# One list of SBUF places for z, its sums and its split parts, with splits issued five steps ahead, in a fused attention and two-FFN kernel

## The chip, the cores and the metric

The kernel runs on one core of one Trainium2 chip. The metric is device microseconds (us) of one execution. TensorE (PE in the profile; PEld is its weight load) multiplies, VectorE (DVE) and ScalarE (ACT) do the elementwise work, SyncE (SP) issues nearly all DMAs. Every engine runs its own instructions in program order.

## The reference

```
attn: x (8,8,512,64), state (8,8,32,64)
  xread = softmax(x @ state.T / 8) @ state ; sread = softmax(state @ x.T / 8) @ x
  tokens = concat(xread, sread) per batch: 8 x (512 + 32) = 4352 rows of 512
moe:  h = tokens @ w_in (512x2048); y = leaky_relu(h, 0.01) @ w_out (2048x512)
moe2: z = silu(y @ w_gate) * (y @ w_val)   (512x1536 each)
      out = z @ w_out2                     (1536x512), 4352 x 512 float32
```

## The kernel before

**Layer 1** (up to 695 us) does attention and the first FFN for eight blocks of 512 tokens and one tail block of 256 state rows, and leaves y in DRAM. Beside it, `convert` and `finish2` prepare the second FFN's weights: `stage` loads a 512 KB tile of 64-bit words (`ws`), `to_f32` turns it into float32 (`two`), `finish2` forms sums of quadrants and splits each value into a high and a low part (`hl`), which go to `quad_dram`. For w_out2 (key "o") `stage` issues four DMAs, which also reorder the columns in runs of 32.

**Layer 2** handles the blocks in four pairs (i, j). All products are float32 values as high and low parts, three matmuls for a product of two 128-wide pieces (`multiply` or `passes`: low x high, high x low, high x high). A pair's matrix product is done by seven products in place of eight (steps p, s, q, b, r, a, c of sums of quadrants), and each has two stages:

- `quads(f)`, f = 0 to 5 (HF = 6): the gate and value products of the column tiles f and f + 6, from `yc` (the sums of y, split), 13 steps in the order ORDER2; each step is 6 matmuls. `keep` (ACT) copies a bank to a temporary C, `add` (DVE, L801) adds a bank to it, `gate_out` and `val_out` make z. `last_product(f)` is step c of gate and value; its matmuls continue in the bank X of steps p, q, r, so they wait until `add` of step r has read that bank. `z_sum` makes sums of z (u).
- `read_out`: out = z @ w_out2, 42 steps (seven steps times six f), 6 matmuls each. `split_next(n + 2)` issues the split (`split_h` on ACT makes zh, `split_l` on DVE makes zl) of the operand that step n + 2 multiplies; zh and zl have three buffers each. Where a chain ends (f = 5), the two banks are copied to C (p, s, q), or, for b, r, a, added to C (two DVE adds) and turned by two 32x32-block transposes into `ost`, which four DMAs store; for c the banks are turned directly. Step n = 0 is followed by `last_product(5)`.

`y_sums` makes the next pair's `yc`: it loads y (`yr`), and on each call makes one to three casts (ACT), differences and low parts (DVE). In `read_out`, `others(n)` calls it at every second step (the third read-out at most steps before 28, then `tail`). `Places` is a list of SBUF tags: `take` uses the oldest free one, `give` returns it. The weights `wq` are loaded 16 places ahead by SP.

The order of all engines is the order in which this code issues.

Of the kernel before, what the change touches and what calls it, by code (L numbers as in the profile page):

```python
# [25 lines left out]
def kernel(  # L26
# [612 lines left out]
    def y_sums(pair, take, give):  # L639
# [32 lines left out]
        for k in range(2):  # L672
            b = raw_b[k]
            high(0, k, b["B0"])
            t4 = sub(b["B3"], b["B0"])
            yield
            high(1, k, b["B1"])
            low(0, k, b["B0"])
            yield
            high(2, k, b["B2"])  # L680
            t6 = sub(b["B2"], b["B3"], b["B3"])
            yield
            high(4, k, t4)
            low(2, k, b["B2"], False)
            yield
            t5 = sub(b["B2"], t4, b["B2"])
            high(6, k, t6)
            if k == 0:
                raw_b.append({"B0": load(i, 1), "B3": load(j, 1)})
            yield  # L690
            high(5, k, t5)
            low(4, k, t4)
            yield
            low(1, k, b["B1"], False)
            t7 = sub(b["B1"], t5, b["B1"])
            if k == 0:
                raw_b[1] |= {"B1": load(i, 3), "B2": load(j, 3)}
            yield
            high(7, k, t7)
            low(5, k, t5)  # L700
            yield
            low(6, k, t6)
            low(7, k, t7)
            yield
# [3 lines left out]
    ORDER3 = "psqbrac"  # L708

    def order_of_products():  # L710
        for p in pairs:
# [10 lines left out]
            for step in ORDER3:  # L722
                for f in range(HF):
                    yield "o", f, step
                    if (step, f) == (ORDER3[0], 0):
                        yield from (("gate", HF - 1, "c"), ("val", HF - 1, "c"))
# [19 lines left out]
    def layer2(p2, ps2):  # L746
# [30 lines left out]
        Zt, Zu = {}, {}  # L777

        def z_sum(n, f):

            if n == 0:
                Zu[f] = p2.tile([P, 2, S], F32, tag=f"u{f}", name="u", bufs=1)
            t1, t2 = Zu[f][:, 0], Zu[f][:, 1]
            i, j = Zt[f][:, 0], Zt[f][:, 1]
            i2, j2 = (Zt[f + HF][:, 0], Zt[f + HF][:, 1]) if n else (None, None)
            out, a, b = [(t1, j, i), (t2, j2, t1), (j, j2, j), (t2, i2, t2)][n]
            nc.vector.tensor_tensor(out=out, in0=a, in1=b, op=ALU.subtract)

        def z_operand(step, f):
            return {  # L790
                "p": Zt[f][:, 0], "s": Zu[f][:, 0], "q": Zu[f][:, 1], "b": Zt[f + HF][:, 1],
                "r": Zt[f][:, 1], "a": Zt[f + HF][:, 0], "c": Zu[f][:, 1],
            }[step]
# [15 lines left out]
        def val_out(sg, c, f, half):  # L809
            if f not in Zt:  # L810
                Zt[f] = p2.tile([P, 2, S], F32, tag=f"z{f}", name="z", bufs=1)
            nc.vector.tensor_tensor(out=Zt[f][:, half, :], in0=c, in1=sg[0], op=ALU.mult)
# [66 lines left out]
        def split_z(key, src):  # L879
            z = zs[key] = tuple(p2.tile([P, S], F32R, tag=t, name=t, bufs=3) for t in ("zh", "zl"))  # L880
            split_h(z[0], src)
            split_l(z[1], src, z[0])
# [3 lines left out]
        def split_next(n):  # L886
            if n < len(order_o):
                step, f = order_o[n]
                split_z((step, f), z_operand(step, f))
                if step == "q":  # L890
                    z_sum(3, f)
# [3 lines left out]
        def quadrant_out(block, half, parts, tags, store):  # L895

            o = wres.tile([P, S // 32, 2, 32], F32, tag=f"wr{14 + stored[0] % 2}", name="ost", bufs=1)
            stored[0] += 1
            for d, src in enumerate(parts):
                nc.vector.transpose(out=o[:, :, d, :], in_=src)  # L900
            for q in range(4):
                c = half * 256 + 64 * q
                store[q % len(store)].dma_start(
                    out=out[block * SB:block * SB + S, c:c + 64].rearrange("(g t) c -> t g c", t=32),
                    in_=o[32 * q:32 * (q + 1)].rearrange("t g d c -> t g (d c)"),
                )
# [16 lines left out]
        def read_out(p, others):  # L923

            i, j = pairs[p]
            B_, K = {}, {}
            for n, (step, f) in enumerate(order_o):
                split_next(n + 2)
                w, tag = weights_of("o", f, step)
                zh, zl = zs.pop((step, f))  # L930
                chain_of = {"q": "p", "r": "p", "c": "p", "b": "s"}.get(step, step)
                if chain_of not in B_:
                    B_[chain_of] = [banks.take("ps_o") for _ in range(2)]
                for d in range(2):

                    wh, wl = w[:, 0, d * P:(d + 1) * P], w[:, 1, d * P:(d + 1) * P]
                    todo = [(wl, zh), (wh, zl), (wh, zh)]
                    for m, (a, v) in enumerate(todo):
                        nc.tensor.matmul(  # L939
                            B_[chain_of][d][0], lhsT=a, rhs=v, start=chain_of == step and f == 0 and m == 0,  # L940
                            stop=step in "abc" and f == HF - 1 and m == 2, skip_group_check=True,
                        )
                used(tag)
                if n == 0:
                    last_product(HF - 1)
                    z_sum(1, HF - 1)
                    z_sum(2, HF - 1)
                if f == HF - 1:
# [3 lines left out]
                    elif step == "c":  # L952
                        last = p + 1 == len(pairs)
                        quadrant_out(i, 1, bank, (), (nc.sync, nc.scalar) if last else (nc.sync,))
                    else:
                        kept = K.pop({"a": "p", "b": "q", "r": "s"}[step])
                        for c, t in zip(kept, bank):
                            add(c, t)
                        block, half = {"a": (i, 0), "b": (j, 0), "r": (j, 1)}[step]
                        quadrant_out(block, half, [c for c, _ in kept], (), (nc.sync,))  # L960
                        temps.give(*(t for _, t in kept))
                    if step in "abc":
                        banks.give(*(t for _, t in B_.pop(chain_of)))
                if n:
                    others(n)

        def tail():
# [35 lines left out]
            y = []  # L1003
            for k in range(2):
                t, tag = yr[k]
                parts = p2.tile([P, 2, 2 * n], F32R, tag=f"z{k}", name="yt", bufs=1)
                split_h(parts[:, 0, :], t)
                split_l(parts[:, 1, :], t, parts[:, 0, :])
                temps.give(tag)
                y += [(parts[:, 0, d * n:(d + 1) * n], parts[:, 1, d * n:(d + 1) * n]) for d in range(2)]  # L1010
# [13 lines left out]
            def hidden(f):  # L1024
# [14 lines left out]
                z = zs[f, 2] = tuple(p2.tile([P, S], F32R, tag=t, name=t, bufs=3) for t in ("zh", "zl"))  # L1039
                split_h(z[0][:, :n], sg[:, :n])  # L1040
                split_l(z[1][:, :n], sg[:, :n], z[0][:, :n])
# [10 lines left out]
            for f in range(NF2):  # L1052
# [7 lines left out]
                zh, zl = zs.pop((f, 2))  # L1060
# [6 lines left out]
                wtiles[0].give(*tags)  # L1067
                load2("o", f + 2)
                if f + 2 >= NF2:
                    held[0] = False  # L1070
# [6 lines left out]

        def first_z():
            for n in range(2):
                yield  # L1080
                split_next(n)

        for p in range(len(pairs)):
# [3 lines left out]
            for f in range(HF):  # L1087
# [3 lines left out]
                quads(f, first_z() if f == HF - 1 else iter(()))  # L1091
            tail_steps = tail() if p + 2 == len(pairs) else iter(())

            def others(n):
                if p + 2 == len(pairs):
                    if n < 28:
                        for _ in range(1 if n % 8 else 0):
                            next(sums_y, None)
                    elif n < 39:
                        next(tail_steps)  # L1100
                elif n % 2:
                    next(sums_y, None)

            read_out(p, others)
            for kept in (Zt, Zu):
                kept.clear()
# [3 lines left out]
    with tc.manual_schedule():  # L1110
# [64 lines left out]
        def finish2():  # L1175
# [4 lines left out]
            for m in range(len(keys2) // 2):  # L1180
# [5 lines left out]
                if kind == "o":  # L1186
                    a = [t[:, 0, 0:256], t[:, 1, 0:256], t[:, 0, 256:512], t[:, 1, 256:512]]
                    raws = [t[:, :, 0:256], t[:, :, 256:512]]
# [5 lines left out]

                def sums(out, x, y, op=ALU.subtract):
                    nc.vector.tensor_tensor(out=out, in0=x, in1=y, op=op)
# [17 lines left out]
                for n, two_raw in zip((0, 2), raws):  # L1214
                    hl = halves()
                    split_h(hl[:, :, 0].bitcast(F32R), two_raw)
                    yield 0.05
                    split_l(hl[:, :, 1].bitcast(F32R), two_raw, hl[:, :, 0])
# [350 lines left out]
```

## Time and profile before

| | |
|---|---|
| median of three executions | 1462.88 us (1462.82 to 1463.76) |
| profiled execution | 1462.61 us, of which 1460.8 us span |
| granted TensorE clock, mean | 0.999 of full speed (2.4 GHz) |
| layer 1, to the first product of layer 2 | 0 to 695.8 us |
| layer 2: stages of one pair, quads / read-out | 111.5 us / 66.4 us |
| the second FFN on the tail block | 1229.5 to 1281 us |

A row of a group tells count (x), busy time and mean; a row of the timeline tells start, length, engine, line, operation, what it writes and reads, and in brackets how long the engine sat idle before it and which instruction ended that wait. Lines are those of the kernel before.

### The profile page before, as it was taken

What the parts mean: (1) busy time and instruction counts of PE and PEld (TensorE: products, weight loads), DVE (VectorE), ACT (ScalarE), POOL (GpSimd) and SP (SyncE); (2) the same over time, 40 slices, a digit from 0 to 9 for tenths busy, and PEclk for the clock granted to TensorE, in tenths of its full rate; (3) what the DMA queues carried; (4) which work ended last, traced back from release to release, by engine and by line L of the source; (5) the groups of instructions that cost most, each with busy time, mean ns of one, the idle gap of its engine ahead of it and who ended that gap; (6) DMA issues with size and microseconds to landing.
All of it is one profiled execution on the core that took longest, in us unless ns stands there. A gap on an engine that the chain in (4) does not pass through costs nothing.

```text
span 1460.8 us, 21155 instructions
## 1 busy us (share of the span) xinstructions
PE 1417.8 (97%) x7386; PEld 1123.2 (77%) x7386; DVE 971.0 (66%) x1721; ACT 742.0 (51%) x1335; POOL 3.0 (0%) x8
## 2 busy tenths in 40 slices
PE   5999999999999999999999999999999999999998
PEld 1445777777777777888888778887788878988876
DVE  6877678676777685543555875558665697545575
ACT  6877656666656565644433543336433364333353
POOL 0000000000000000000000000000000000000000
PEclk9999999999999999999999999999999999999999
DMA  8895656667666765551667676676866767876664
GB/s 288 296 317 194 216 203 243 208 223 237 224 219 225 197 188 187 202 181 37 213 193 222 208 218 206 194 224 206 222 203 194 222 198 217 253 262 194 193 187 112
DMA packets 213593, 307.59 MB, mean 211 GB/s; under 512 B 73840, under 2 KB 100464, under 8 KB 212464
## 3 DMA queue, kind: packets, MB, share of 16 engines
q1 hardware_dynamic: 211280, 297.60, 64.9%
q10 hardware_dynamic: 2208, 8.65, 1.5%
q8 instruction: 59, 0.97, 0.3%
q14 instruction: 46, 0.38, 0.1%
HBM read 225.44 MB, written 80.74 MB: 210 GB/s over the span
## 4 chain that ended last, share of the span: by engine, by line
PE 82%; DVE 10%; ACT 3%; DMA 3%; issue 1%; SPq 1%; DVEq 0%; ACTq 0%
PE ps_y L451 22%; PE ps_x L770 16%; PE ps_h L451 13%; PE ps_s L770 9%; PE ps_o L939 9%; PE ps_a L770 4%; DVE zl L167 3%; PE ps_t L451 2%; PE ps_sw L475 2%; DVE C L801 2%; PE ps_yt L451 2%; ACT zh L164 1%; PE ps_s L326 1%; PE ps_o L451 1%; DVE ost L900 1%
## 5 line engine op out<-in xcount | busy, mean ns | idle before, releaser
L451 PE MATMUL ps_y<-gh,w_parts 128*128 128x512 f32 x1024 | 339.7, 392 | 0.0
L770 PE MATMUL ps_x<-yc,wq 128*128 128x512 f32 x1152 | 279.2, 390 | 3.2 <-DVE C L801 3.2
L770 PEld LDWEIGHTS ps_x<-yc,wq 128*128 128x128 f32 x1152 | 215.9, 188 | 49.4 <-DVE C L801 4.9
L451 PEld LDWEIGHTS ps_y<-gh,w_parts 128*128 128x128 f32 x1024 | 192.2, 188 | 52.1 <-issue 7.6
L939 PE MATMUL ps_o<-zh,wq 128*128 128x512 f32 x672 | 208.8, 390 | 0.0
L451 PE MATMUL ps_y<-gl,w_parts 128*128 128x512 f32 x512 | 199.4, 389 | 0.0
L167 DVE TENSOR_TENSOR gl<-hs,gh 128x512 fp32r<-128x512 f32 (+1 forms) x144 | 95.1, 660 | 113.4 <-ACT gh L164 113.2
L567 ACT ACTIVATE hs<-ps_h 128x512 f32<-128x512 f32 (+1 forms) x144 | 82.7, 574 | 155.4 <-PE ps_h L451 154.0
L770 PE MATMUL ps_s<-yc,wq 128*128 128x512 f32 x576 | 146.1, 389 | 0.0
L939 PEld LDWEIGHTS ps_o<-zh,wq 128*128 128x128 f32 x672 | 126.2, 188 | 25.7
L939 PE MATMUL ps_o<-zl,wq 128*128 128x512 f32 x336 | 134.1, 399 | 10.0 <-DVE zl L167 9.5
L805 ACT ACTIVATE sg<-C 128x512 f32<-128x512 f32 x72 | 45.5, 632 | 157.6 <-DVE C L801 157.6
L770 PEld LDWEIGHTS ps_s<-yc,wq 128*128 128x128 f32 x576 | 108.2, 188 | 22.4
L451 PEld LDWEIGHTS ps_y<-gl,w_parts 128*128 128x128 f32 x512 | 96.2, 188 | 19.6
L451 PE MATMUL ps_h<-ah,swl 128*128 128x512 f32 x256 | 106.4, 416 | 3.5 <-ACT hs L567 2.4
L797 ACT COPY C<-ps_x 128x512 f32<-128x512 f32 x96 | 56.0, 583 | 102.4 <-PE ps_x L770 102.4
L451 PE MATMUL ps_h<-al,swh 128*128 128x512 f32 x256 | 100.0, 390 | 1.4 <-DVE al L167 1.4
L451 PE MATMUL ps_h<-ah,swh 128*128 128x512 f32 x256 | 100.3, 392 | 0.0
L801 DVE TENSOR_TENSOR C<-ps_s,C 128x512 f32<-128x512 f32 x48 | 33.2, 691 | 99.8 <-PE ps_s L770 99.4
L939 PEld LDWEIGHTS ps_o<-zl,wq 128*128 128x128 f32 x336 | 63.0, 188 | 33.6 <-DVE zl L167 21.2
L164 ACT CAST zh<-z 128x512 fp32r<-128x512 f32 x96 | 59.1, 621 | 57.1 <-PE ps_o L939 44.6
L164 ACT CAST gh<-hs 128x512 fp32r<-128x512 f32 (+1 forms) x144 | 85.7, 595 | 3.0
(137 smaller groups left out, 2115.3 us busy)
## 6 DMA issues: line engine op xcount, KB each, us to landing
wq<-quad_gate SPq DMA_DIRECT2D x168, 256.0 KB
wq<-quad_val SPq DMA_DIRECT2D x168, 256.0 KB
wq<-quad_o SPq DMA_DIRECT2D x168, 256.0 KB
ws<-in_dram SPq DMA_DIRECT2D x56, 512.0 KB
sw<-sw_dram SPq DMA_DIRECT2D x56, 256.0 KB
quad_gate<-hl SPq DMA_DIRECT2D x24, 512.0 KB
quad_val<-hl SPq DMA_DIRECT2D x24, 512.0 KB
quad_o<-hl SPq DMA_DIRECT2D x24, 512.0 KB
```

The lines of the kernel that those rows point to most:

```text
L164: nc.scalar.copy(dst, src)
L167: nc.vector.tensor_tensor(out=dst, in0=src, in1=hi.bitcast(F32), op=ALU.subtract)
L326: nc.tensor.matmul(ps[2 * NS * i:2 * NS * (i + 1)], lhsT=states[:, p, b, :], rhs=xt.pop((b, p)), start=True, stop=True,)
L451: nc.tensor.matmul(ps, lhsT=w, rhs=v, start=first and n == 0, stop=last and n == len(todo) - 1)
L475: nc.tensor.matmul(ps[e], lhsT=flat[half, p, 4 * bs:4 * bs + 4, :].rearrange("d b n -> d (b n)"), rhs=raw["in", g, p][half], start=True, s ...
L567: nc.scalar.activation(hs, ps[:, :n], AF.Prelu, alpha=0.01)
L770: nc.tensor.matmul(bank, lhsT=a, rhs=v, start=first and n == 0, stop=last and n == len(todo) - 1, skip_group_check=True,)
L797: nc.scalar.copy(t[0], src)
L801: nc.vector.tensor_tensor(out=kept[0], in0=bank, in1=kept[0], op=ALU.add)
L805: nc.scalar.activation(t[0], c, AF.Sigmoid)
L900: nc.vector.transpose(out=o[:, :, d, :], in_=src)
L939: nc.tensor.matmul(B_[chain_of][d][0], lhsT=a, rhs=v, start=chain_of == step and f == 0 and m == 0, stop=step in "abc" and f == HF - 1 and ...
```

## The change

1. **Places.** z, u (z's sums) and zh, zl all come from one list `zt` of 42 places of 128x512 (before: 12 + 6 tiles of two, and three buffers each for zh and zl). A z is given back right after its split, zh and zl after their matmuls.
2. **Splits.** `split_next(n + 5)` instead of n + 2; the first five are issued in `quads(1)` to `quads(5)` at step 7, no longer two in `quads(5)`.
3. **One per step.** A chain's adds and transposes, and the third z sums, become jobs: each step of `read_out` issues one piece of a job, or else one call of `y_sums`. `y_sums` is recut so that each call holds one DVE instruction (22 calls a pair instead of 18), and its first five calls move into `quads(5)`, steps 8 to 12.
4. `last_product(5)` comes after step n = 1 instead of n = 0.
5. In the last read-out, step c multiplies all six f into the first bank, then all six into the second; each bank is turned and stored by itself (eight DMAs of 128-byte runs instead of four of 256).
6. `stage` loads w_out2 by whole rows, one DMA; `finish2` reads the columns through a strided view instead, and splits such a half in two instructions of 256 instead of one of 512.

```diff
@@ stage
-        if key[0] == "o":
-            for h in range(2):
-                for d in range(2):
-                    nc.sync.dma_start(
-                        out=t[:, 256 * h + 128 * d:256 * h + 128 * (d + 1)].rearrange("p (q c) t -> p q (c t)", q=4),
-                        in_=src[:, 512 * h:512 * (h + 1)].rearrange("p (q d c) -> p d q c", d=2, q=4)[:, d],
-                    )
-        elif len(src.shape) == 2:
+        if len(src.shape) == 2:
             nc.sync.dma_start(out=t.rearrange("p c t -> p (c t)"), in_=src)
@@ layer2
+        Z = {}
+        zt = Places(p2, [f"z{n}" for n in range(6 * HF + 6)], [P, 512])
...
+        def split_z(step, f):
+            src, tag = Z[f, OPERAND[step]]
+            zs[step, f] = (h, _), (l, _) = [zt.take(name, dtype=F32R) for name in ("zh", "zl")]
+            split_h(h, src)
+            split_l(l, src, h)
+            if step != "q":
+                zt.give(tag)
@@ quads
+                if f and n == 7:
+                    split_next(f - 1)
@@ read_out
+            def added(step, block, half):
+                kept = K.pop({"a": "p", "b": "q", "r": "s"}[step])
+                chain_of = {"b": "s", "r": "p"}.get(step, step)
+                bank = B_[chain_of]
+                for c, (t, _) in zip(kept, bank):
+                    add(c, t)
+                    yield
+                if step != "r":
+                    banks.give(*(t for _, t in B_.pop(chain_of)))
+                yield from quadrant_out(block, half, [c for c, _ in kept], (nc.sync,))
+                temps.give(*(t for _, t in kept))
...
             for n, (step, f) in enumerate(order_o):
-                split_next(n + 2)
+                split_next(n + AHEAD)
...
-                if n == 0:
+                zt.give(zh[1], zl[1])
+                if n == 1:
                     last_product(HF - 1)
...
                 if n:
+                    if not next_job():
+                        next(steps, None)
                     others(n)
@@ after quads
-                quads(f, first_z() if f == HF - 1 else iter(()))
+                quads(f, sums_y if f == HF - 1 else iter(()))
```

The change moves instructions at three places that matter below. The first is VectorE at the end of the first pair's `quads(5)`. Before, from the multiplication by the sigmoid (sg) of step ga to the add that frees the value bank (last row):

```order
L806 TENSOR_TENSOR sg_8063<-C_7974,sg_8063 128x512
L167 TENSOR_TENSOR zl_8077<-z_7287,zh_8076 128x512
L801 TENSOR_TENSOR C_8074<-ps_s_8020,C_8074 128x512
L812 TENSOR_TENSOR z_8089<-C_8074,sg_8050 128x512
L167 TENSOR_TENSOR zl_8092<-z_7445,zh_8091 128x512
L801 TENSOR_TENSOR C_8017<-ps_a_8095,C_8017 128x512
L812 TENSOR_TENSOR z_8089<-C_8017,sg_8063 128x512
L801 TENSOR_TENSOR C_7985<-ps_x_7965,C_7985 128x512
L806 TENSOR_TENSOR sg_8115<-C_7985,sg_8115 128x512
L787 TENSOR_TENSOR u_8118<-z_8089 128x512
L801 TENSOR_TENSOR C_8029<-ps_x_8008,C_8029 128x512
```

After, from the second of the moved `y_sums` calls (the first, a T, and the same sg stand right ahead of it) to the same add:

```order
L167 TENSOR_TENSOR yc_8089<-yr_7974,yc_8089 128x512
L791 TENSOR_TENSOR C_8101<-ps_s_8039,C_8101 128x512
L801 TENSOR_TENSOR z_8115<-C_8101,sg_8069 128x512
L657 TENSOR_TENSOR yr_7976<-yr_7980,yr_7976 128x512
L791 TENSOR_TENSOR C_8036<-ps_a_8118,C_8036 128x512
L801 TENSOR_TENSOR z_8128<-C_8036,sg_8086 128x512
L167 TENSOR_TENSOR yc_8104<-T_8091,yc_8104 128x512
L791 TENSOR_TENSOR C_8002<-ps_x_7982,C_8002 128x512
L796 TENSOR_TENSOR sg_8142<-C_8002,sg_8142 128x512
L167 TENSOR_TENSOR yc_8130<-yr_7980,yc_8130 128x512
L781 TENSOR_TENSOR u_8148<-z_8115,z_8128 128x512
L791 TENSOR_TENSOR C_8048<-ps_x_8027,C_8048 128x512
```

The two splits (zl) have left this stretch, and five instructions of `y_sums` (T, yc, yr, yc, yc) have come into it.

The second is VectorE in the first pair's read-out where chain b ends (C from ps_o is the add, ost the transpose, zl a split). Before:

```order
L167 TENSOR_TENSOR yc_8449<-yr_8297,yc_8449 128x512
L167 TENSOR_TENSOR zl_8481<-z_7287,zh_8480 128x512
L167 TENSOR_TENSOR zl_8493<-z_7445,zh_8492 128x512
L801 TENSOR_TENSOR C_8419<-ps_o_8245,C_8419 128x512
L801 TENSOR_TENSOR C_8421<-ps_o_8246,C_8421 128x512
L900 STREAM_TRANSPOSE ost_8506<-C_8419 128x16x32
L900 STREAM_TRANSPOSE ost_8506<-C_8421 128x16x32
L665 TENSOR_TENSOR yr_8299<-yr_8364,yr_8299 128x512
L167 TENSOR_TENSOR zl_8517<-z_7603,zh_8516 128x512
L167 TENSOR_TENSOR zl_8529<-z_7761,zh_8528 128x512
```

After:

```order
L167 TENSOR_TENSOR yc_8498<-yr_8214,yc_8498 128x512
L167 TENSOR_TENSOR zl_8529<-z_7935,zh_8528 128x512
L791 TENSOR_TENSOR C_8452<-ps_o_8286,C_8452 128x512
L167 TENSOR_TENSOR zl_8542<-z_8115,zh_8541 128x512
L791 TENSOR_TENSOR C_8454<-ps_o_8287,C_8454 128x512
L167 TENSOR_TENSOR zl_8555<-z_7355,zh_8554 128x512
L902 STREAM_TRANSPOSE ost_8566<-C_8452 128x16x32
L167 TENSOR_TENSOR zl_8569<-z_7520,zh_8568 128x512
L902 STREAM_TRANSPOSE ost_8566<-C_8454 128x16x32
L167 TENSOR_TENSOR zl_8582<-z_7685,zh_8581 128x512
```

Adds and transposes no longer stand four in a row; a split stands behind each of them.

The third is SP late in layer 1, around the last of the twelve w_out2 tiles (ws), the load that the prediction speaks of. Before:

```order
L1213 DMA quad_o_135<-hl 128x1024
L1220 DMA quad_o_135<-hl 128x1024
L525 DMA sw<-sw_dram_1_143 128x1x512
L199 DMA ws<-in_dram 128x4x64 x4
L1220 DMA quad_o_135<-hl 128x1024
L525 DMA sw<-sw_dram_2_144 128x1x512
L1210 DMA quad_o_136<-hl 128x1024
L525 DMA sw<-sw_dram_2_144 128x1x512
```

After:

```order
L1269 DMA quad_o_135<-hl 128x1024
L1279 DMA quad_o_135<-hl 128x1024
L517 DMA sw<-sw_dram_1_143 128x1x512
L196 DMA ws<-in_dram 128x1024
L1279 DMA quad_o_135<-hl 128x1024
L517 DMA sw<-sw_dram_2_144 128x1x512
L1266 DMA quad_o_136<-hl 128x1024
L517 DMA sw<-sw_dram_2_144 128x1x512
```

Each of the w_out2 loads is one DMA of 128 rows instead of four in pieces of 64 words; nothing else has moved here.

## Rows read from the trace of the kernel before

**Rows 1.** The page, part 1: busy time of each engine.
```profile
PE 1417.8 (97%) x7386; PEld 1123.2 (77%) x7386; DVE 971.0 (66%) x1721; ACT 742.0 (51%) x1335; POOL 3.0 (0%) x8
```

**Rows 2.** Busy time by stretch: first pair's quads, then the four read-outs.
```profile
core 0: us, PE busy (x) PEld busy (x) DVE busy (x) ACT busy (x) POOL busy (x), PEclk, DMA share, GB/s
695.76:807.30 111.54, 111.54 (x494) 92.41 (x493) 63.66 (x98) 38.41 (x67) 0.00 (x0) 1.00 0.69 212
807.30:873.70 66.40, 61.88 (x265) 49.00 (x264) 56.61 (x91) 36.20 (x62) 0.00 (x0) 1.00 0.73 214
985.22:1051.67 66.45, 61.93 (x265) 49.02 (x264) 56.66 (x91) 36.18 (x62) 0.00 (x0) 1.00 0.73 213
1163.19:1229.53 66.34, 63.35 (x265) 48.55 (x264) 58.78 (x95) 38.73 (x67) 0.00 (x0) 1.00 0.70 206
1392.53:1454.95 62.42, 61.27 (x265) 48.99 (x263) 44.09 (x69) 29.11 (x48) 0.00 (x0) 1.00 0.54 152
```

**Rows 3.** The waits of TensorE: us in total, times, longest.
```profile
PE ps_o L939 <- DVE zl L167: 9.5, 16, 1.3
...
PE ps_x L770 <- DVE C L801: 3.2, 4, 0.8
PE ps_h L451 <- ACT hs L567: 2.4, 2, 2.1
```

**Rows 4.** Timeline of TensorE, first read-out.
```profile
807.30 0.39 PE L939 MATMUL ps_o<-zh,wq 128*128 128x512 f32 x1
...
808.66 1.52 PE L770 MATMUL ps_x<-yc,wq 128*128 128x512 f32 x6
810.99 1.66 PE L770 MATMUL ps_x<-yc,wq 128*128 128x512 f32 x6 [0.80 <-DVE C L801]
...
849.38 0.50 PE L939 MATMUL ps_o<-zl,wq 128*128 128x512 f32 x1 [0.72 <-DVE zl L167]
...
868.35 0.50 PE L939 MATMUL ps_o<-zl,wq 128*128 128x512 f32 x1 [1.32 <-DVE zl L167]
```

**Rows 5.** Timeline of VectorE around the ends of chains b and a.
```profile
845.66 1.28 DVE L801 TENSOR_TENSOR C<-ps_o,C 128x512 f32<-128x512 f32 x2
846.86 1.29 DVE L900 STREAM_TRANSPOSE ost<-C 128x512 f32<-128x512 f32 x2
848.08 0.65 DVE L665 TENSOR_TENSOR yr<-yr 128x512 f32<-128x512 f32 x1
848.65 1.28 DVE L167 TENSOR_TENSOR zl<-z,zh 128x512 fp32r<-128x512 f32 x2
...
867.61 1.89 DVE L167 TENSOR_TENSOR zl<-u,zh 128x512 fp32r<-128x512 f32 x3
```

**Rows 6.** Timeline of VectorE at the end of the first pair's quads.
```profile
802.80 0.69 DVE L806 TENSOR_TENSOR sg<-C,sg 128x512 f32<-128x512 f32 x1 [0.70 <-ACT sg L805]
...
804.40 0.68 DVE L801 TENSOR_TENSOR C<-ps_s,C 128x512 f32<-128x512 f32 x1
805.12 0.69 DVE L812 TENSOR_TENSOR z<-C,sg 128x512 f32<-128x512 f32 x1
...
807.65 0.68 DVE L801 TENSOR_TENSOR C<-ps_x,C 128x512 f32<-128x512 f32 x1
809.03 0.69 DVE L806 TENSOR_TENSOR sg<-C,sg 128x512 f32<-128x512 f32 x1 [0.70 <-ACT sg L805]
...
810.25 0.69 DVE L801 TENSOR_TENSOR C<-ps_x,C 128x512 f32<-128x512 f32 x1
```

**Rows 7.** Timeline of SP and ACT: w_out2 load in layer 1; first load of all.
```profile
1.66 0.42 SPq L204 DMA_DIRECT2D ws<-in_dram  x1
6.93 0.67 ACT L221 ACTIVATE ws<-ws 128x512 f32<-128x512 f32 x1
571.71 4.53 SPq L199 DMA_DIRECT2D ws<-in_dram  x4
580.95 0.65 ACT L221 ACTIVATE ws<-ws 128x512 f32<-128x512 f32 x1 [7.75 <-DMA ws<-in_dram]
581.51 0.58 ACT L567 ACTIVATE hs<-ps_h 128x512 f32<-128x512 f32 x1
```

**Rows 8.** Timeline of the SP queue: loads of y for the second pair.
```profile
788.88 1.79 SPq L645 DMA_DIRECT2D yr<-y_dram  x4
```

**Rows 9.** Timeline at the end of the program.
```profile
1454.47 1.40 DVE L900 STREAM_TRANSPOSE ost<-ps_o 128x512 f32<-128x512 f32 x2 [2.05 <-PE ps_o L939]
...
1454.72 0.39 PE L939 MATMUL ps_o<-zh,wq 128*128 128x512 f32 x1
1455.89 0.85 SPq L903 DMA_DIRECT2D out_dram<-ost  x2
```

More of the change, by code (lines that the diff above doesn't have):

```diff
@@ L776, in layer2 @@
         X, Ys, Zs, U, C, SG = {}, {}, {}, {}, {}, {}
-        Zt, Zu = {}, {}
+        Z = {}
+        zt = Places(p2, [f"z{n}" for n in range(6 * HF + 6)], [P, 512])
         def z_sum(n, f):
-            if n == 0:
[L782 to L793, printed above, removed]
+            if n < 2:
+                Z[f, "st"[n]] = zt.take("u")
+            out, a, b = [("s", "j", "i"), ("t", "j2", "s"), ("j", "j2", "j"), ("t", "i2", "t")][n]
+            nc.vector.tensor_tensor(out=Z[f, out][0], in0=Z[f, a][0], in1=Z[f, b][0], op=ALU.subtract)
+        OPERAND = {"p": "i", "s": "s", "q": "t", "b": "j2", "r": "j", "a": "i2", "c": "t"}
         def keep(name, src):
@@ L809, in val_out @@
         def val_out(sg, c, f, half):
-            if f not in Zt:
-                Zt[f] = p2.tile([P, 2, S], F32, tag=f"z{f}", name="z", bufs=1)
-            nc.vector.tensor_tensor(out=Zt[f][:, half, :], in0=c, in1=sg[0], op=ALU.mult)
+            Z[f % HF, "ij"[half] + "2" * (f // HF)] = z, _ = zt.take("z")
+            nc.vector.tensor_tensor(out=z, in0=c, in1=sg[0], op=ALU.mult)
             temps.give(sg[1])
@@ L933, in read_out @@
                     B_[chain_of] = [banks.take("ps_o") for _ in range(2)]
-                for d in range(2):
[L936 to L942, printed above, removed]
+                if zh is None:
+                    held_c.append(w)
+                    if f == HF - 1:
+                        finish_jobs()
+                        ends = quadrant_out(i, 1, [t for t, _ in B_["p"]], (nc.sync, nc.scalar), True)
+                        for d in range(2):
+                            for k, w in enumerate(held_c):
+                                multiply(w, [z for z, _ in zs["c", k]], B_["p"][d][0], d, False, k == HF - 1)
+                            next(ends)
+                        list(ends)
+                    else:
+                        next_job()
+                    continue
+                for d in range(2):
+                    multiply(w, (zh[0], zl[0]), B_[chain_of][d][0], d, chain_of == step and f == 0, step in "abc" and f == HF - 1)
                 used(tag)
-                if n == 0:
+                zt.give(zh[1], zl[1])
+                if n == 1:
                     last_product(HF - 1)
@@ L952, in read_out @@
                     elif step == "c":
-                        last = p + 1 == len(pairs)
-                        quadrant_out(i, 1, bank, (), (nc.sync, nc.scalar) if last else (nc.sync,))
-                    else:
[L956 to L963, printed above, removed]
+                        jobs.append(quadrant_out(i, 1, bank, (nc.sync,)))
+                    else:
+                        jobs.append(added(step, *{"a": (i, 0), "b": (j, 0), "r": (j, 1)}[step]))
                 if n:
+                    if not next_job():
+                        next(steps, None)
                     others(n)
+            finish_jobs()
+            banks.give(*(t for _, t in B_.pop("p")))
         def tail():
@@ L1090, in layer2 @@
                     next(sums_y)
-                quads(f, first_z() if f == HF - 1 else iter(()))
+                quads(f, sums_y if f == HF - 1 else iter(()))
             tail_steps = tail() if p + 2 == len(pairs) else iter(())
             def others(n):
[L1095 to L1106, printed above, removed]
+                if p + 2 == len(pairs) and 28 <= n < 39:
+                    next(tail_steps)
+            read_out(p, others, sums_y)
+            Z.clear()
             list(sums_y)
```

137 lines of the change are left out of this document (93 added, 44 removed).

## The prediction

> **What bounds the kernel now.** I read four views, in this order. The page first: TensorE is busy in 97% of the span, VectorE in 66%, ScalarE in 51% [rows 1], so only TensorE's idle time and its order can be worth anything, and what VectorE does counts only where TensorE waits for it. Then busy time by stretch, to find where the missing 3% lie: the quads run without a gap (111.54 us busy in 111.54), and the four read-outs do not [rows 2]. Then TensorE's waits, which name the cause: in layer 2 it waits for zl, the low parts of z, and at one place in each pair for the DVE add into C; the third row, hs, is a place late in layer 1 [rows 3]. Last the timelines of TensorE and VectorE around these waits [rows 4 to 6].
>
> The price of the read-outs comes from two of the views. One step of six matmuls takes 1.36 us (807.30 to 808.66 [rows 4]), a matmul 0.2267 us. A read-out with its `last_product` has 264 of them, 59.84 us. The four took 66.40, 66.45, 66.34 and 62.42 us [rows 2]: 6.56, 6.61, 6.50 and 2.58 too long, **22.25 us in all**. Of each, about 1.1 lie at the value half of `last_product`: it should start at 808.66 + 1.36 = 810.02, starts at 810.99, and the matmul behind it runs 0.13 late once more (1.66 us instead of 1.52) [rows 4]. The rest are waits for zl. Their cause can be read at 849.38: VectorE ran two adds, two transposes and a y sum from 845.66 to 848.73 and only then the split of the next step [rows 5]. That is 3.0 us of other work in front of a split that is issued two steps, 2.7 us, ahead. At 868.35 the same with two y sums costs 1.32 us [rows 4].
>
> **The change, term by term.**
>
> *Splits five steps ahead, one job a step (the waits for zl).* Five steps are 6.8 us. In the changed order each step of the first pair's read-out holds one split and at most one more VectorE instruction. Three such instructions in a row took 1.89 us where one takes 0.69 [rows 5], so they start 0.60 apart, two in 1.20 us, against 1.36 for TensorE's step. VectorE then gains 0.15 us a step instead of falling back by 3.0 at a chain's end, and a chain's add that has to wait for its bank is followed at once by a split that is not needed for five steps. I take these waits as gone. The cover is the five steps; were only two left, the present 0.7 to 1.3 us for each chain end would come back.
>
> *The trace against a rule here.* A lone DVE instruction of 512 float32 takes 0.69 us, but the next starts 0.60 us after it [rows 5]. The Trainium skill, "VectorE: DVE Perf Modes", section "The DRAIN you can't avoid", says that the next instruction does not start until the pipe is empty, which would space them by the full 0.69; by that rule two a step are 1.38 us and the read-out would be bound by VectorE (rival B has its time). The rows differ from the rule, and the sum goes by the rows.
>
> *`last_product` one step later, five y sums earlier (the add into C).* This is a wait that does not go. In the first three pairs five `y_sums` instructions now stand before the add that frees the value bank, and two splits no longer do. From [rows 6]: independent instructions 0.60 apart, a multiplication on the add before it 0.72 (804.40 to 805.12), a multiplication across the sigmoid 1.38 (807.65 to 809.03). The multiplication at 802.80 comes 0.60 later, since the split for step 4 now stands in front of ga's add: 803.40. From there the changed order has T, yc, add (1.80), z (0.72), yr, add (1.20), z (0.72), yc, add (1.20), the multiplication across the sigmoid (1.38), yc, u, add (1.80): 8.82 us, so the last add starts at 812.2 and ends at 812.9; before it ended at 810.94. TensorE, with one step more in between, wants to go on at 810.02 + 1.36 = 811.38. It waits 1.6 us, with the late matmul 1.7, instead of 1.1. The gate half needs gr's add, which ends at 809.7, before 810.02. Behind it the split for step 7 is the ninth instruction and done near 818.5; step 7 starts near 821, so nothing else is late. In the fourth pair there are no y sums: the add is 3.0 us earlier, no wait. So of the 22.25 us, **3 x 1.7 = 5.1 stay and 17.1 go**. Bounds for this term: if the add came in time, 22.25 go; if VectorE needed the full 0.69 for each instruction, the add would be about 0.9 us later in each of three pairs, and 14.4 go.
>
> *The places.* 42 before in tiles of fixed use, 42 now. At the start of a read-out three are free; each step takes two, and gets back one from the split's source (not in step q) and two from the matmuls. A split thus takes places whose matmuls lie two to three steps back, while it runs five ahead; ScalarE, which writes zh first, now waits for steps long past. Cost nothing; if a place came only from the step in progress, four steps of lead would be left.
>
> *w_out2 by whole rows.* Late in layer 1 ScalarE stood still 7.75 us for such a load, from its first issue at 571.71 to 580.95, 9.24 us, and TensorE behind it for hs: two waits, 2.1 and 0.3 us [rows 3, 7]. The load's four DMAs kept SP for 4.53 us; one of whole rows was issued in 0.42, and the first of all was in use 5.27 us after its issue (1.66 to 6.93), in company of others [rows 7]. If the load takes under 9.24 - 2.14 = 7.1 us, the large wait goes whole; at 5.27 it does. I take **-2.1**, with bounds 0 (something else on the queues is what is slow) and -2.4 (both go). The Trainium skill, "DMA: Bandwidth & Descriptors", section "Specifications", puts line rate at 512 bytes and more; the four DMAs had 256-byte pieces, and the wait agrees with the rule without proving it. The strided halves in `finish2` cost one more instruction on each of ACT and DVE for 12 halves; at 0.69 each some 8 us of engines with a third or more of the span to spare [rows 1], behind which TensorE's stretch has no gap.
>
> *The end.* The last transposes already overlap: the one of the second bank starts as the last matmul ends and both are done at 1455.87 [rows 9]. Now the second bank alone is turned and stored, in pieces half as long, by the same number of DMAs on each queue; the first bank's stores go out 3.4 us earlier. From the last issue to the end nothing in the trace prices 128-byte pieces: between no gain and the 0.85 us of two issues either way; I take 0.
>
> **Sum** against the profiled execution: 1462.61 - 17.1 - 2.1 = 1443.4. The median of the runs shown is 0.27 above that execution, so **1443.7 us**.
>
> **The rivals.**
>
> A. *The add comes in time* (VectorE catches up between products): all 22.25 and 2.1 go, 1438.5. Against it speaks that the add was 0.97 late before, with fewer instructions ahead of it [rows 4, 6]. Chance 0.09.
>
> B. *VectorE is the bound in the read-outs* (instructions 0.69 apart): the add 0.9 later in three pairs, and 2 x 0.69 = 1.38 a step, which loses 0.02 a step and is hidden by the lead: 1446.4; with a lost lead on top about 1448. The three in 1.89 us speak against it [rows 5]. This is what the section of the Trainium skill named above would make of the kernel. Chance 0.09.
>
> C. *The lead is there in the order but not in time*: VectorE enters each read-out late by the five y sums, and waits for zl remain at half their number: 17.1 becomes about 8.5, 1452.3. Against it: the 2.5 us that are left at step 7, growing. Chance 0.05.
>
> D. *Nothing is gained*: the time that zl costs turns into an equal wait for another engine, 1462.9. TensorE shows no other waits in these stretches [rows 3]. Chance 0.03.
>
> E. *Slower.* The first y sum now stands on VectorE's queue in front of the add of vb, at 804.0 us, and waits there for y's loads, with every add and split behind it. The loads were issued from 788.88 to 790.67 [rows 8], 13 us earlier. To eat the gain of 19.2 us, three pairs would have to wait 6.4 us each, that is loads landing 20 us after their issue; the slowest load above took 9.24 to its use [rows 7]. With loads of 25 us: three times 11, 1477. Chance 0.03.
>
> **How the numbers follow.** The forecast has 0.71. About 0.2% (2.9 us) is what a measurement of this kernel can tell from no change. Faster by more than that: forecast, A, B, C, 0.94, less a little for an unknown cost in layer 1's moved DMAs: 0.93. Within it 0.04, slower 0.03. The range 1438.5 to 1449 holds the forecast with its bounds (the add 14.4 to 22.25, the load 0 to 2.4, the end 0.85), A's edge and B; C, D and E, 0.11, lie outside with the tails.
>
> **What would show it.** TensorE's row for zl should vanish from its waits; the row for the add into C should have three waits (one in each of the first three pairs) of about 1.6 us instead of four of 0.8; the read-outs should take about 61.6 us three times and 59.8 once; the row for hs should lose its 2.1. Three steps can fail: the 0.60 us spacing (then C's wait is over 2 us), the lead (then zl's row stays), and the load (then ScalarE's long wait for ws stays). Read-outs over 63 us would prove the forecast wrong.

## The result, and the profile of the changed kernel

The changed kernel takes **1444.91 us** (median of four, 1444.50 to 1445.33) against 1463.32 of the kernel before on the same chip: ratio 0.9867, 95% interval 0.9847 to 0.9888. 1443.7 was predicted. The profiled execution took 1445.33 us with a span of 1443.2, where before's were 1462.61 and 1460.8.

Busy time by stretch of the changed kernel: the first pair's quads, then the four read-outs (columns as in [rows 2]).

```profile
694.09:807.43 113.34, 111.85 (x494) 92.27 (x493) 68.61 (x107) 43.28 (x76) 0.00 (x0) 1.00 0.68 209
807.43:869.09 61.66, 60.14 (x266) 49.47 (x265) 52.71 (x86) 29.86 (x56) 0.00 (x0) 1.00 0.76 223
980.61:1042.27 61.66, 60.18 (x265) 49.47 (x264) 52.68 (x86) 29.85 (x56) 0.00 (x0) 1.00 0.74 222
1153.79:1215.47 61.68, 60.20 (x266) 49.48 (x265) 55.08 (x90) 32.85 (x61) 0.00 (x0) 1.00 0.74 220
1378.43:1438.27 59.84, 59.84 (x265) 49.36 (x263) 39.83 (x65) 24.44 (x45) 0.00 (x0) 1.00 0.59 162
```

Against [rows 2] the read-outs lost 4.74, 4.79, 4.66 and 2.58 us, 16.8 in all. But the first quads, which had run without a gap in 111.54 us, now take 113.34. TensorE's waits say where both come from (two rows of that view; all others lie in the first 200 us):

```profile
PE ps_x L766 <- DVE C L791: 4.5, 3, 1.5
...
PE ps_x L766 <- ACT yst L599: 1.5, 1, 1.5
```

The rows for zl (9.5 us) and for hs (2.4 us) of [rows 3] are gone. The wait for the add into C is there three times, 1.5 us each. The wait for `yst` is new. The timelines of VectorE and TensorE show the first C wait, where [rows 4, 6] showed it before:

```profile
804.14 0.68 DVE L657 TENSOR_TENSOR T<-yr 128x512 f32<-128x512 f32 x1
804.74 0.68 DVE L167 TENSOR_TENSOR yc<-yr,yc 128x512 fp32r<-128x512 f32 x1
...
811.25 0.68 DVE L167 TENSOR_TENSOR yc<-yr,yc 128x512 fp32r<-128x512 f32 x1
811.85 0.69 DVE L781 TENSOR_TENSOR u<-z 128x512 f32<-128x512 f32 x1
812.45 0.68 DVE L791 TENSOR_TENSOR C<-ps_x,C 128x512 f32<-128x512 f32 x1
```
```profile
810.15 1.52 PE L766 MATMUL ps_x<-yc,wq 128*128 128x512 f32 x6
813.19 1.66 PE L766 MATMUL ps_x<-yc,wq 128*128 128x512 f32 x6 [1.52 <-DVE C L791]
```

The add starts at 812.45 (the prediction worked out 812.2, for a read-out that starts 0.13 earlier), TensorE is done with the first group at 811.67, waits 1.52 us, and the second group takes 1.66 instead of 1.52. Without the wait that group would have started 1.36 us after the first, at 811.51, so it is 1.68 late and loses 0.14 more in itself: a wait that the view puts at 1.52 costs 1.82. The same 0.3 us on top of the row stand at every other wait that was priced here (0.80 in [rows 4] cost 1.10).

The new wait lies where layer 2 begins. ScalarE's timeline and TensorE's there:

```profile
690.81 2.64 ACT L599 COPY yst<-ps_y 128x512 f32<-128x512 f32 x4 [4.05 <-PE ps_y L443]
...
693.84 1.14 ACT L164 CAST yc<-yr 128x512 fp32r<-128x512 f32 x2 [0.40 <-ACT yst L599]
695.95 1.14 ACT L164 CAST yc<-yr 128x512 fp32r<-128x512 f32 x2 [0.96 <-DVE yr L657]
697.28 0.62 ACT L164 CAST yc<-yr 128x512 fp32r<-128x512 f32 x1 [0.19 <-DVE yr L657]
697.80 1.19 ACT L599 COPY yst<-ps_yt 128x256 f32<-128x256 f32 x4
```
```profile
695.48 1.52 PE L766 MATMUL ps_s<-yc,wq 128*128 128x512 f32 x6
698.49 1.66 PE L766 MATMUL ps_x<-yc,wq 128*128 128x512 f32 x6 [1.49 <-ACT yst L599]
```

Between the last block's copy and the tail's (the small `yst` from `ps_yt`) stand five casts for `yc`, three of them behind VectorE's differences. The third product of layer 2 takes the bank that the tail's copy frees, and waits 1.49 us.

**Where the 17.6 us of span come from** (start times of the same matmuls in both traces): the first 60 us are 1.3 longer; from there to layer 2 is 3.0 shorter; the first quads 1.8 longer; the read-outs 16.8 shorter; the end 0.9 shorter; the other stretches agree within 0.05. 1.3 - 3.0 + 1.8 - 16.8 - 0.9 = -17.6.

### The profile page after: what moved, and what is told of

It is laid out like the page before. It is cut to its first block, busy times and chain, and to the rows that moved or that the text cites. A ratio compares the mean times of both kernels' runs of the same rounds, so it can differ in the third digit from the quotient of the medians.

```text
span 1443.2 us, 21041 instructions
## 1 busy us (share of the span) xinstructions
PE 1412.3 (98%) x7386; PEld 1126.0 (78%) x7386; DVE 965.6 (67%) x1733; ACT 731.3 (51%) x1347; POOL 3.0 (0%) x8
## 4 chain that ended last, share of the span: by engine, by line
PE 93%; DVE 3%; ACT 2%; DMA 1%; issue 1%; ACTq 0%; SPq 0%; DVEq 0%
PE ps_y L443 24%; PE ps_x L766 17%; PE ps_o L967 15%; PE ps_h L443 14%; PE ps_s L766 9%; PE ps_a L766 4%; PE ps_t L443 2%; PE ps_sw L467 2%; PE ps_yt L443 1%; PE ps_o L443 1%; PE ps_s L318 1%; DVE C L791 1%; PE ps_r L415 1%; ACT sw L473 1%; PE ps_sw L455 0%
## 5 line engine op out<-in xcount | busy, mean ns | idle before, releaser
L967 PE MATMUL ps_o<-zl,wq 128*128 128x512 f32 x336 | 130.7, 389 | 0.0
L443 PEld LDWEIGHTS ps_y<-gl,w_parts 128*128 128x128 f32 x512 | 96.1, 188 | 19.8
L796 DVE TENSOR_TENSOR sg<-C,sg 128x512 f32<-128x512 f32 x72 | 49.9, 693 | 50.5 <-ACT sg L795 50.5
```

The source lines that it names most:

```text
L443: nc.tensor.matmul(ps, lhsT=w, rhs=v, start=first and n == 0, stop=last and n == len(todo) - 1)
L796: nc.vector.tensor_tensor(out=t[0], in0=c, in1=t[0], op=ALU.mult)
L967: nc.tensor.matmul(bank, lhsT=a, rhs=v, start=start and m == 0, stop=stop and m == 2, skip_group_check=True,)
```

## The experiments

Medians in us; "ratio" is to the kernel before on the same chip (before's medians there: 1464.1 to 1465.1). The waits are TensorE's in layer 2, in total and times. The first two rows are for comparison.

| kernel | median | ratio (95%) | for zl | for C | for yst |
|---|---|---|---|---|---|
| before | 1463.32 | 1 | 9.5, 16 | 3.2, 4 | none |
| changed | 1444.91 | 0.9867 (0.9847 to 0.9888) | none | 4.5, 3 | 1.5 |
| 1: lead of two steps | 1448.60 | 0.9894 (0.9879 to 0.9909) | 3.6, 4 | 2.8, 3 | 1.5 |
| 2: chain ends in a row | 1445.40 | 0.9870 (0.9856 to 0.9883) | none | 4.5, 3 | 1.5 |
| 3: 1 and 2 | 1451.33 | 0.9912 (0.9899 to 0.9926) | 5.1, 8 | 2.8, 3 | 1.5 |
| 4: before, load by rows | 1460.94 | 0.9973 (0.9960 to 0.9986) | 9.6, 16 | 3.2, 4 | none |
| 5: no early y sums | 1439.33 | 0.9825 (0.9811 to 0.9838) | none | none | 1.5 |
| 6: `last_product` later | 1439.55 | 0.9827 (0.9813 to 0.9840) | none | none | 1.5 |
| 7: tail's y first | 1442.94 | 0.9849 (0.9836 to 0.9863) | none | 4.5, 3 | none |
| 8: old end | 1447.13 | 0.9877 (0.9863 to 0.9890) | none | 4.5, 3 | 1.5 |
| 9: 3 with old y sums | 1453.58 | 0.9926 (0.9913 to 0.9939) | 7.5, 17 | none | none |
| 10: 5 and 7 | 1437.31 | 0.9813 (0.9799 to 0.9828) | none | none | none |
| 11: 10, low parts twice | 1506.31 | 1.0287 (1.0270 to 1.0304) | 32.2, 109 | none | none |
| 12: 9 with a lead of five | 1437.16 | 0.9815 (0.9801 to 0.9828) | none | none | none |

### What covers the splits (1, 2, 3, 9, 12)

**Run 1**, splits two steps ahead:

```diff
-    AHEAD = 5
+    AHEAD = 2
...
-                if f and n == 7:
+                if 0 < f <= AHEAD and n == 7:
```


> The changed kernel with splits issued two steps ahead instead of five; one piece per step stays. Theory of the prediction (the lead of five steps is the cover): the waits for zl come back at the chain ends, 0.7 to 1.3 us each, about 12 us in all, 1457 us. Rival (one piece per step is enough): at a chain end a split now stands behind each add, so no wait there; only the multiplications and sums that last_product puts on VectorE stand in front of the split of step 4, about 1.5 us in each pair, 1451 us.

**Run 2**, a chain's adds and transposes in a row:

```diff
+                if f == HF - 1:
+                    finish_jobs()
                 if n:
                     if not next_job():
```


> The changed kernel with a chain's two adds and two transposes issued in a row at its end; five steps of lead stay. Theory of the prediction (the lead is the cover): 3.0 us of other work in front of a split that has 6.8 us to spare, so no wait for zl and the same time as the changed kernel, 1444.9 us within 0.5. Rival (one piece per step does it): waits for zl of 0.7 us at three chain ends of each pair, about 1452 us.

**Run 3**, both:

> The changed kernel with both undone: two steps of lead, and a chain's adds and transposes in a row. Both theories: the waits for zl of the kernel before come back, 12 to 17 us, 1457 to 1462 us. If it stays under 1450 us, neither the lead nor the spreading was what took these waits away, and the one list of places or the recut y sums would have to be.

Run 2 came out as the prediction's theory has it, run 1 nearest to its rival (1451, 2.4 too high), run 3 at neither forecast. VectorE's timeline in run 1 where chain b ends (its first add at 844.93) shows why a lead of two steps is enough there: behind each add and transpose stands a split.

```profile
844.33 0.69 DVE L167 TENSOR_TENSOR zl<-z,zh 128x512 fp32r<-128x512 f32 x1
844.93 0.69 DVE L791 TENSOR_TENSOR C<-ps_o,C 128x512 f32<-128x512 f32 x1
845.53 0.68 DVE L167 TENSOR_TENSOR zl<-z,zh 128x512 fp32r<-128x512 f32 x1
846.13 0.68 DVE L791 TENSOR_TENSOR C<-ps_o,C 128x512 f32<-128x512 f32 x1
```

Run 1's waits for zl are elsewhere: once in each of the first three pairs at step 4, behind `last_product` (a fourth, of 0.2 us, lies in the last read-out). Both sums of z and a y sum come before that split:

```profile
814.66 0.69 DVE L801 TENSOR_TENSOR z<-ps_x,sg 128x512 f32<-128x512 f32 x1
815.27 0.68 DVE L781 TENSOR_TENSOR u<-z,u 128x512 f32<-128x512 f32 x1
815.87 0.69 DVE L781 TENSOR_TENSOR z<-z 128x512 f32<-128x512 f32 x1
816.47 0.68 DVE L657 TENSOR_TENSOR yr<-yr,T 128x512 f32<-128x512 f32 x1
817.08 0.68 DVE L167 TENSOR_TENSOR zl<-z,zh 128x512 fp32r<-128x512 f32 x1
```
```profile
817.82 0.50 PE L967 MATMUL ps_o<-zl,wq 128*128 128x512 f32 x1 [1.14 <-DVE zl L167]
```

That makes 1.4 us a pair with the late matmuls. In return the C wait fell to 0.9 each, since no split stood in front of it. Run 3 adds only four waits, 1.5 us in all, to those of run 1, so something else had to hold the rest. **Run 9** puts the y sums and the third z sums back too (the old 18 calls, none in `quads(5)`, at the old steps):

```diff
-                    jobs.append(z3(f))
+                    z_sum(3, f)
...
-                    if not next_job():
-                        next(steps, None)
+                    next_job()
...
+                elif n % 2:
+                    next(sums_y, None)
```


> As the run with two steps of lead and bunched chain ends, and now also the y sums as before (18 calls of one to three differences and low parts, at every second step, at most steps in the third read-out) and the third z sums at once instead of one per step. Theory: it was these that held the rest of what the two other measures did not give back; TensorE waits for zl some 16 times again, 9 us or more, and the time is that of the kernel before less the load and the end, about 1460 us. Rival (the one list of places, or the first splits at their new positions, took the waits away): it stays at 1452 us or less.

Seventeen waits for zl are back, 7.5 us: the recut y sums and the z sums spread over the steps did hold the rest; the run does not tell which of the two. The time was 6.4 us below the forecast of 1460: 4.4 are the four C waits of before with their late matmuls, 1.1 each, which this kernel does not have and which I had not taken off, and about 2 the somewhat shorter waits for zl. **Run 12** is run 9 with `AHEAD = 5`, the only one of the three measures left:

> As the run before with the old y sums, the bunched chain ends and no y sums in quads(5), but with five steps of lead instead of two: of the three measures only the lead is left. Theory of the prediction (the lead is the cover, the rest is not needed): no wait for zl in any read-out, no wait for the add into C and none at the start of layer 2, so the time of the kernel with both fixes, 1437.3 us within 1. Rival (where up to three differences and low parts, the third z sum and a split fall into one step, VectorE falls back by more than 6.8 us, in the third read-out above all): some waits stay, 1441 us or more.

1437.16 us, with all four read-outs at the 59.84 us of their matmuls:

```profile
806.16:866.00 59.84, 59.84 (x266) 49.55 (x264) 52.51 (x87) 31.90 (x59) 0.00 (x0) 1.00 0.76 221
977.52:1037.36 59.84, 59.84 (x266) 49.55 (x264) 52.51 (x87) 31.90 (x59) 0.00 (x0) 1.00 0.76 221
1148.88:1208.72 59.84, 59.84 (x266) 49.55 (x264) 55.10 (x91) 34.95 (x64) 0.00 (x0) 1.00 0.74 221
1371.70:1431.54 59.84, 59.84 (x265) 49.36 (x263) 40.03 (x65) 24.45 (x45) 0.00 (x0) 1.00 0.58 162
```

The lead alone, of these three, takes every wait for zl away. It needs the one list of places, which holds five steps' split parts and was there in run 9 too, where these waits were only 2.0 us shorter in all than before. Issuing one piece per step is a second, partial cover for the same thing, and on top of the lead it gains nothing.

### What the C wait is made of (5, 6)

**Run 5** leaves the y sums out of `quads(5)`; **run 6** moves `last_product(5)`:

```diff
-                quads(f, sums_y if f == HF - 1 else iter(()))
+                quads(f, iter(()))
```
```diff
-                if n == 1:
+                if n == 3:
                     last_product(HF - 1)
```


> The changed kernel without y sums in quads(5); all 22 calls run in the read-out, which has 23 steps without a job. Theory: the five y sums in front of the adds make the wait for the add into C; without them VectorE is 3 us earlier, the three waits of 1.5 us and the three late matmuls go, and nothing takes their place: 5.3 us, 1439.6 us. Rival (the wait comes from the chain of sigmoid and multiplication between the adds): the wait shrinks by at most half, 1442 us or more.

> The changed kernel with last_product(5) after step n = 3 instead of n = 1. Theory: TensorE wants the value bank 2.7 us later, the add that ends 1.5 us late is then in time: 5.3 us, 1439.6 us. Rival (the work behind it is late instead): the sums of z that follow last_product come 2.7 us later on VectorE, and a wait for zl or for a bank takes the place, at least 1441.5 us.

Both theories held within 0.3 us. The C wait is made by the five y sums, and two steps more of distance hide it as well. The y sums could have been had for nothing: in the read-out (run 5), or perhaps (not tried) a little earlier in `quads(5)`, where VectorE sat idle 3.55 us in the changed kernel:

```profile
799.54 0.69 DVE L791 TENSOR_TENSOR C<-ps_s,C 128x512 f32<-128x512 f32 x1 [3.55 <-PE ps_s L766]
```

### Layer 1 and the end (4, 7, 8)

**Run 4** is the kernel before with part 6 of the change alone:

> The kernel before with only the load of w_out2 by whole rows and the strided views in finish2 that go with it. Theory: ScalarE's wait of 7.75 us for ws goes and with it both waits of TensorE for hs, 2.4 us or a little more: 1460.6 us; no new wait at the start of layer 2, since the y sums of the first pair are not recut here. Rival (what is won is given back at the start of layer 2 whatever the y sums): TensorE waits there about 1.5 us for the copy of the tail's y, and the time is 1462 to 1463 us.

Both waits for hs went, and no wait for `yst` came. Over the two places themselves run 4 gains 3.06 us and the changed kernel 3.05 (the same matmuls of `ps_y`, at 560.40 and 583.86 us in the kernel before): 2.14 and 0.31 us of wait, and 0.3 more behind each. Elsewhere ahead of layer 2 run 4 lost 0.7 us, whose cause stays open, so layer 2 starts 2.3 us earlier than before. By medians it is 3.3 us, and the interval allows 2.0 to 5.9.

**Run 7**:

```diff
-        list(sums0)
         y_out(B)
+        list(sums0)
```


> The changed kernel with the copies of the tail's y issued before what is left of the first pair's y sums at the end of layer 1. Theory: the recut into 22 calls left five casts instead of two in front of these copies on ScalarE, and the bank that they free was 1.5 us late; now the bank is free at about 695.3 us, before it is wanted at 696.9, and 1.6 us go: 1443.3 us. Rival (the casts are needed as early as that): the wait moves to a product of the first quads, and the time stays at 1444.9 us.

The tail's copies (first row of the operation's statistics: duration, first and last start) moved ahead of the casts, nothing waits for them, and the first quads are back at 111.5 us:

```profile
L599 ACT COPY yst<-ps_yt x4: 367/382/397, 693.9 to 694.7; 128x256 f32<-128x256 f32 x4
```

**Run 8** undoes part 5 (two lines: step c is multiplied f by f into both banks, and the last stores go out as before):

> The changed kernel with the end of the last read-out as before: step c multiplies each f into both banks, both are turned, four stores of 256-byte runs on SP and ACT. Theory: the 0.9 us by which the program ends sooner after its last matmul (4.93 us now, 5.85 before) come from this part: 1445.8 us. Rival (they come from elsewhere, or are chance): 1444.9 us, and 4.9 us from the last matmul to the end.

From the start of the last matmul to the end of the span it takes 6.2 us (1439.65 to 1445.9), the changed kernel 5.1 (1438.05 to 1443.2), the kernel before 6.1 [rows 9]. So the 0.9 is this part's. The rest of the 2.2 us between the medians is not: the kernel before, run beside each of them, differs by 1.7 us as well (1465.05 against 1463.32), and in the profiled execution layer 2, ahead of which nothing was edited, started 1.7 us later. The timelines at the end, of run 8 and then of the changed kernel:

```profile
1439.40 1.40 DVE L902 STREAM_TRANSPOSE ost<-ps_o 128x512 f32<-128x512 f32 x2 [5.06 <-PE ps_o L967]
...
1439.65 0.39 PE L967 MATMUL ps_o<-zh,wq 128*128 128x512 f32 x1
...
1440.83 0.85 SPq L896 DMA_DIRECT2D out_dram<-ost  x2
```
```profile
1438.05 0.39 PE L967 MATMUL ps_o<-zh,wq 128*128 128x512 f32 x1
1438.47 0.72 DVE L902 STREAM_TRANSPOSE ost<-ps_o 128x512 f32<-128x512 f32 x1 [3.36 <-PE ps_o L967]
```

In both the last transpose ends about 1.15 us after the last matmul starts. So the gain lies behind it, in the stores: four follow the last transpose in either kernel, and each of them now carries half the bytes.

### Both fixes, and VectorE's room (10, 11)

> The changed kernel without y sums in quads(5) and with the copies of the tail's y first at the end of layer 1. Theory: the two gains lie at different places and add, 5.6 and 2.0 us as measured: 1437.5 us, no wait of TensorE in layer 2 but one of less than 0.1 us. Rival (one of them only moves a wait that the other removes as well): 1439 us.

1437.31 us: the two gains add. This kernel and run 12 beat both kernels of the case, by 7.6 us and 27 us. **Run 11** issues each `split_l` of a split a second time:

```diff
             split_l(l, src, h)
+            split_l(l, src, h)
```


> The kernel with both fixes, and every low part of a split computed twice, the second time with the same result: three VectorE instructions a step instead of two. If they start 0.60 us apart, as the rows of before show, a step costs VectorE 1.80 us against TensorE's 1.36, the lead of five steps is used up, and TensorE waits some 12 us in each of the first three read-outs and not in the fourth, which has no y sums: 1473 us. If each takes its full 0.69 us, about 22 us three times and 7 us in the fourth: 1511 us. If VectorE has room for three, 1437.5 us.

1506.31 us: neither forecast of the spacing. VectorE's timeline shows a third value:

```profile
826.63 1.41 DVE L167 TENSOR_TENSOR zl<-u,zh 128x512 fp32r<-128x512 f32 x2
827.96 0.69 DVE L657 TENSOR_TENSOR yr<-yr 128x512 f32<-128x512 f32 x1
828.56 1.41 DVE L167 TENSOR_TENSOR zl<-u,zh 128x512 fp32r<-128x512 f32 x2
```

The two low parts take 1.41 where two independent ones take 1.28 or 1.29 [rows 5]: the second, which writes the tile that the first has just written, starts 0.72 after it; everything else in these rows starts 0.60 to 0.61 after the one before. A step is 1.93 us, 0.57 more than TensorE's. The read-outs took 78.4, 78.4, 79.0 and 69.9 us, 18.5, 18.5, 19.2 and 10.1 too long: my 12 and 0 had two low parts at 1.20, and counted on the whole lead. The view's row has only 32.2 us for these waits, but they are 109: at 0.3 us more for each they make 65 of the 66.3 us. How much of the lead is used up before the first wait was not taken apart.

## Why the prediction was right, and where it was not

- **Splits five steps ahead: right.** Of 22.25 us, 16.8 went (17.1 predicted), no wait for zl is left, and the fourth read-out has the 59.84 us foretold. Run 12 shows that the lead is the cover, as the prediction put it. What it said for a lead of two steps, that 0.7 to 1.3 us for each chain end would come back, was wrong for this kernel: the splits that stand behind adds and transposes cover the ends too (run 1), and what came back was the split behind `last_product`, which it had only costed at five steps.
- **The add into C: right in mechanism and place, 0.1 us small.** Three waits of 1.48 to 1.52 us and late matmuls make 1.82 a pair against 1.7; 5.5 stay instead of 5.1, and none in the fourth pair. Run 5 shows that it is the five y sums.
- **The 0.60 us spacing (rival B): right.** The add came where that spacing puts it, and VectorE's timeline in run 3 has six low parts in a row in 3.67 us, 5 x 0.60 and one of 0.68:

```profile
849.44 3.67 DVE L167 TENSOR_TENSOR zl<-z,zh 128x512 fp32r<-128x512 f32 x6
```

  The sentence that the prediction cites from the Trainium skill, "VectorE: DVE Perf Modes", section "The DRAIN you can't avoid", would by itself give 6 x 0.69 = 4.1; run 11's step would be 2.07 by it, and is 1.93. But the same section goes on, "A next op that is not held starts earlier", which the prediction left out: with it the section allows the 0.60 of these rows, and rival B had less behind it than the prediction gave it.
- **The places: right.** In the first read-out of the kernel before, ScalarE's writing of zh waited 26 times for TensorE, 19.8 us in all; in the changed kernel it does so not once.
- **w_out2 by whole rows: right in mechanism, too small.** 2.1 was predicted with bounds to 2.4, and 3.05 measured at the place, in run 4 and the changed kernel alike. Both waits went, not the larger alone, and the sum had left out the 0.3 us that each costs beyond its row, which the term for the add into C had counted. ScalarE's long wait did not go, as "what would show it" put the test; it fell from 7.75 us to 5.16. The load took 6.6 us to its use, not 5.27, which is still under the 7.1 that mattered:

```profile
572.53 0.33 SPq L196 DMA_DIRECT2D ws<-in_dram  x1
```
```profile
579.12 0.67 ACT L213 ACTIVATE ws<-ws 128x512 f32<-128x512 f32 x1 [5.16 <-DMA ws<-in_dram]
```

- **A step that was missing: the recut of `y_sums` was costed in layer 2 alone.** The sum has no term for the first pair's y sums, which run in layer 1 at a fixed pace. With 22 calls instead of 18, seven are left for its end instead of three, and five casts instead of two stand ahead of the tail's copies on ScalarE: 1.8 us in the first quads, shown by run 7. The order of ScalarE at that place could have told it.
- **The end: 0.9 us gained** where 0 was taken, just past the bound of 0.85 (run 8).
- **The start: 1.3 us lost**, in code that the change does not touch (below). In sum: 0.3 less from the read-outs, 1.8 and 1.3 lost unforeseen, 0.9 more from the load and 0.9 from the end: 1.6 less gained than the 19.2 of the sum, against the profiled execution's span. That the total came out so near is in part luck: 3.4 us were missed one way and 1.8 the other.

None of the rivals came: A's 1438.5 needed the add in time, and C's lost lead and E's late loads do not show in TensorE's waits. Of D, another wait in place of the old, there is a little: the wait for `yst`, which cost 1.8 us outside the read-outs.

## What to carry to other kernels

State a lead in microseconds of the other engine's work: here 6.8 us of lead covered every bunch of 3 us, and evening the bunches out gained nothing more. Price a wait with what runs late behind it: here each cost 0.3 us beyond the time in its row, some 33 us for the 109 waits of run 11. Work moved to fill an engine's order costs what stands behind it: the five y sums were free in the read-out and cost 5.5 us just ahead of the add that TensorE waits for. When a shared generator is cut into more calls, look at each place that calls it at a fixed pace, since the remainder lands somewhere.

## What was not expected of the hardware

The granted clock differed early in the program, in the same code. Windows of 10 us from 10 to 40 us, of the kernel before and then of the changed one (columns as in [rows 2]):

```profile
10.00:20.00 10.00, 5.41 (x10) 1.26 (x10) 5.54 (x10) 7.04 (x12) 0.00 (x0) 1.00 0.45 169
20.00:30.00 10.00, 8.62 (x25) 2.72 (x24) 9.83 (x21) 7.01 (x14) 0.00 (x0) 1.00 0.96 319
30.00:40.00 10.00, 7.52 (x28) 4.38 (x28) 9.03 (x18) 9.26 (x18) 0.00 (x0) 1.00 1.03 378
```
```profile
10.00:20.00 10.00, 4.93 (x10) 1.25 (x10) 5.26 (x10) 7.11 (x13) 0.00 (x0) 1.00 0.47 186
20.00:30.00 10.00, 7.91 (x19) 2.25 (x18) 9.83 (x20) 7.03 (x14) 0.00 (x0) 0.82 0.97 308
30.00:40.00 10.00, 9.72 (x31) 4.79 (x28) 8.84 (x18) 8.64 (x17) 0.00 (x0) 0.83 0.99 353
```

Both came from a stretch in which TensorE was busy half the time. In one it stayed at the upper level (2.4 GHz), in the other it ran part of the next 20 us at the lower one (1.2 GHz), and the product that began at 57.83 us began at 59.13. Runs 1, 3, 7, 9 and 11 stayed at 1.00 here; runs 2, 5, 8 and 10 fell to 0.81 to 0.85, run 4 to 0.87 and then 0.96, and runs 6 and 12 were at 0.72 and 0.71 from 10 to 20 us already, all without an edit in this part of the program. The clock is not the whole of it: against the kernel before, the matmul at 59.22 us came 2.5 us later in run 8 and 0.1 in run 4, but also 2.2 later in run 3, which stayed at 1.00. What the clock's share of the 1.3 us is was not taken apart. So up to 2.5 us between two profiles of this kernel can be the start and not the edit.

An instruction of VectorE that writes the tile of the one before it starts 0.72 us after it, an independent one 0.60 (run 11). And stores in pieces of 128 bytes ended the program sooner than half as many of 256 (run 8): at the very end the bytes left behind the last matmul counted more than the size of a piece. The Trainium skill, "DMA: Bandwidth & Descriptors", section "Specifications", puts line rate at 512 bytes and more, so both sizes lie below it; no run here shows what 512 would do.
